# Batch two's v sorted in natural layout and re-tiled through DRAM, with GpSimd holding later loads until x^T is there

## The chip, the cores and the metric

One core of a Trainium2 chip. The metric is the device time of one execution in microseconds (us), as the median of several runs. The kernel before takes 226.36 us (226.34 to 226.47, three runs).

The names in the profiles: PE is TensorE and its matmuls, PEld its weight loads, DVE is VectorE, ACT is ScalarE, POOL is GpSimd, SP is the engine whose queue (the sync queue) issues the other transfers; GpSimd issues the loads. To evict is to copy a matmul's result out of PSUM. A turn, or crossbar transpose, is a DMA that transposes on the way. The granted clock is the share of the full TensorE clock that the trace shows.

## The reference

Block-sorted attention over 4 batches and 8 heads, followed by an FFN with squared ReLU. Cut to what matters:

```python
P = sinkhorn(sort_net)                                  # [B, H, 8, 8], five rounds
k_sorted = einsum('bhij,bhjcd->bhicd', P, k_blocks)     # blocks of 96 tokens, 64 wide
v_sorted = einsum('bhij,bhjcd->bhicd', P, v_blocks)
attn = softmax(q_block @ k_sorted_block.T / 8)          # inside each block of 96
x = (attn @ v_sorted_block)  ->  [3072, 512]            # 4 batches of 768 tokens
out = relu(x @ w_in) ** 2 @ w_out                       # w_in 512x2048, w_out 2048x512
```

## The kernel before

The attention of a batch is interleaved with the FFN of earlier tokens, in an order that a small planner in the program lays out: each piece of work is given engines, an estimated cost and its dependences, and the plan's order becomes the fixed instruction order of each engine. The FFN goes in eight groups of 384 tokens, each of 64 `hp` matmuls (up projection) and 48 `op` matmuls (down projection), or 28 "chunks" of four matmuls. Attention tasks are due at a chunk number.

Batches one and two sort k and v by transposing matmuls and then turn v back with TensorE:

```python
def s_sort(u, t, ...):                 # one tensor of one head pair: 12 matmuls
    nc.tensor.matmul(out=tp[64*h:64*(h+1), a, :], lhsT=src[:, 2*u.hp+h, D*a:D*(a+1)],
                     rhs=w_all[:, H*u.b + 2*u.hp + h, ...])
    ...                                # evict to ksT or vsT (128x768)
def s_vt(u, ...):                      # v alone: 8 transposes, then a copy vs<-vbp
    nc.tensor.transpose(out=vbp[:, n, :], in_=u.vsT[:, ...], identity=ident)
```

Batches three and four sort in natural layout by 32x32 tiles of the array. v then goes to DRAM and back (`v_way`, `vblk`) to get its key blocks; k and q are turned by the DMA crossbar, k from its evicted tile `kn`, q from a copy `qi`:

```python
def s_nat(b, g, t, due):               # one tensor of two head pairs: 16 matmuls
    nc.tensor.matmul(out=p2[slot][32*c:32*(c+1), h, 0:NA*D], lhsT=w_t[r, ...],
                     rhs=src[r, g, NA*D*c:NA*D*(c+1)], tile_position=(r.start, 32*c))
    ...                                # evict to kn (ring of three) or vn; then for v:
    nc.sync.dma_start(out=v_way[b, g]..., in_=vn_r[m]...)
    nc.sync.dma_start(out=vb_r[w]..., in_=v_way[b, g]...)
def s_turn(b, hp):
    nc.sync.dma_start_transpose(out=kx_r[kx]..., in_=kn_r[m]...)
    nc.vector.tensor_copy(out=qi_r[n]..., in_=qkv[b][0][:, 2*hp:2*hp+2, :]...)   # DVE
    nc.sync.dma_start_transpose(out=tiles["qT", b, hp], in_=qi_r[n]...)
```

The inputs of batches three and four are loaded by GpSimd as soon as their buffers (those of two batches before) are free. x^T of batches two to four is made by crossbar too (`xT<-ao`), but for one of batch two's four parts.

The softmax here doesn't subtract the row's maximum and nothing guards it: scores larger than these inputs give would overflow.

## Time and profile before

| | before |
|---|---|
| median of three runs | 226.36 us |
| span of the profiled execution | 224.3 us, granted TensorE clock 1.0 |
| first `hp` matmul starts | 22.3 us |
| last matmul starts | 220.8 us |

### The profile page before, as it was taken

Reading aid. Unit: us, or ns where it says so; the run is one execution under the profiler, and the core shown is the slowest. Engines: PE = TensorE matmul, PEld = TensorE weight load, DVE = VectorE, ACT = ScalarE, POOL = GpSimd, SP = SyncE. Lnnn points to the kernel's source line nnn. Section 1 sums busy time; section 2 is a strip of 40 time slices with the busy share of each in tenths; the row PEclk is TensorE's granted clock in tenths of the full one; section 3 lists DMA queues with packets and bytes.
Section 4 is the critical chain, followed back from the end, with each engine's and each line's share of the span. In section 5 each row is a group of like instructions: output and inputs, shape, how many; then the busy total and the mean of one; then the engine's idle time right before and its main releaser. Section 6 shows DMA issues by size and latency. Waiting matters only on the chain.

```text
span 224.3 us, 5245 instructions
## 1 busy us (share of the span) xinstructions
PE 216.6 (97%) x2130; PEld 122.9 (55%) x2145; DVE 105.7 (47%) x297; ACT 122.1 (54%) x253; POOL 26.4 (12%) x46
## 2 busy tenths in 40 slices
PE   7898999999999999999999999999999999999994
PEld 2476665556665645545665455445665465446553
DVE  6777777317666416640666127523664045005400
ACT  4665776228885328734775248535774177137521
POOL 7962332200004200000000000000000000000000
PEclk9999999999999999999999999999999999999999
DMA  5999999999953996499941320899522410110012
GB/s 66 201 202 208 207 206 205 203 227 245 210 65 27 191 239 145 115 216 201 220 38 35 85 94 0 164 225 254 110 37 43 122 47 1 50 57 37 0 50 94
DMA packets 42744, 28.83 MB, mean 129 GB/s; under 512 B 22752, under 2 KB 38368, under 8 KB 42720
## 3 DMA queue, kind: packets, MB, share of 16 engines
q0 software_dynamic: 13888, 13.63, 37.1%
q1 hardware_dynamic: 28832, 14.86, 29.7%
q8 instruction: 17, 0.28, 0.5%
q14 instruction: 7, 0.06, 0.1%
HBM read 28.89 MB, written 7.91 MB: 164 GB/s over the span
## 4 chain that ended last, share of the span: by engine, by line
PE 92%; DMA 2%; DVE 2%; ACT 1%; issue 1%; ACTq 0%; POOLq 0%
PE hp L810 37%; PE op L838 35%; PE p L550 4%; PE p L731 3%; DMA qb<-in_q_dram 2%; PE p L510 2%; PE qtp L461 2%; PE vbp L598 2%; PE op L872 2%; PE p L350 1%; PE p L632 1%; PE xtp L779 1%; PE tp L510 1%; DVE ao L742 1%; ACT h L818 0%
## 5 line engine op out<-in xcount | busy, mean ns | idle before, releaser
L810 PE MATMUL hp<-xT,w_in_bf 128*128 128x384 bf16 x512 | 91.0, 326 | 0.0
L838 PE MATMUL op<-w_out_bf,h 128*128 128x512 bf16 x353 | 82.6, 379 | 0.8
L818 ACT ACTIVATE h<-hp 128x384 bf16<-128x384 f32 x128 | 62.0, 495 | 23.5 <-PE hp L810 20.0
L821 DVE TENSOR_TENSOR h<-h 128x384 bf16<-128x384 bf16 x128 | 44.5, 355 | 56.3 <-ACT h L818 55.5
L810 PEld LDWEIGHTS <-w_in_bf 128*128 128x128 bf16 x512 | 47.0, 98 | 30.0 <-issue 0.7
L838 PEld LDWEIGHTS <-h 128*128 128x128 bf16 x368 | 34.7, 98 | 39.4 <-issue 0.7
L192 ACT COPY ob<-op 128x512 f32<-128x512 f32 (+1 forms) x25 | 14.2, 569 | 56.0 <-PE op L838 50.6
L742 DVE TENSOR_TENSOR ao<-p,rec 96x512 bf16<-96x512 f32 x32 | 22.0, 687 | 1.4 <-DVE rec L741 0.3
L582 ACT ACTIVATE et<-p 96x384 bf16<-96x384 f32 x48 | 19.4, 491 | 2.4 <-PE p L550 2.4
L741 DVE RECIPROCAL rec<-p 96x8 f32<-96x8 f32 x32 | 6.4, 199 | 13.6 <-PE p L731 13.3
L731 PEld LDWEIGHTS <-et 96*128 96x128 bf16 x256 | 10.6, 97 | 2.9
L261 POOL DMA_DIRECT2D qb<-in_q_dram x8 | 6.0, 754 | 32.5 <-PE qtp L461 24.4
L350 PE MATMUL p<-ones 128*128 128x512 bf16 (+1 forms) x36 | 8.8, 360 | 1.1 <-DVE ones L213 1.1
L194 DVE COPY vs<-vbp 96x512 bf16<-96x512 bf16 (+1 forms) x12 | 6.1, 508 | 7.1 <-PE vbp L598 6.9
L573 ACT ACTIVATE et<-p 96x768 bf16<-96x768 f32 x8 | 6.3, 802 | 2.1 <-PE p L550 2.0
L261 POOL DMA_DIRECT2D kb<-in_k_dram x10 | 6.6, 659 | 6.6 <-DMA w_in_bf<-in_moe_w_in_dram 2.2
L261 POOL DMA_DIRECT2D vb<-in_v_dram x10 | 6.6, 660 | 6.4 <-DMA w_in_bf<-in_moe_w_in_dram 3.6
L192 ACT CAST ksT<-p 128x768 bf16<-128x768 f32 (+1 forms) x7 | 4.6, 662 | 3.3 <-PE p L510 3.3
L550 PEld LDWEIGHTS <-kx 64*128 64x128 bf16 x128 | 4.6, 155 | 2.8 <-issue 2.8
L731 PE MATMUL p<-vs,et 96*128 96x65 bf16 x128 | 6.0, 193 | 0.0
L461 PE MATMUL qtp<-ident,qb 64*64 64x64 bf16 (+1 forms) x144 | 4.7, 204 | 1.3 <-DMA qb<-in_q_dram 1.3
L461 PEld LDWEIGHTS <-qb 64*64 64x64 bf16 (+1 forms) x144 | 3.5, 109 | 4.5 <-DMA qb<-in_q_dram 2.3
(78 smaller groups left out, 129.3 us busy)
## 6 DMA issues: line engine op xcount, KB each, us to landing
out_dram<-ob SPq DMA_DIRECT2D x23, 256.0 KB, 2.8
qb<-in_q_dram POOLq DMA_DIRECT2D x8, 384.0 KB, 15.7
vb<-in_v_dram POOLq DMA_DIRECT2D x6, 384.0 KB, 17.1
kb<-in_k_dram POOLq DMA_DIRECT2D x6, 384.0 KB, 17.1
w_in_bf<-in_moe_w_in_dram POOLq DMA_DIRECT2D x4, 512.0 KB, 12.5
w_out_bf<-in_moe_w_out_dram POOLq DMA_DIRECT2D x4, 512.0 KB, 18.0
v_way<-vn SPq DMA_DIRECT2D x4, 396.0 KB, 4.1
vblk<-v_way SPq DMA_DIRECT2D x4, 396.0 KB, 3.9
```

The lines of the kernel that those rows point to most:

```text
L192: nc.scalar.copy(out=out, in_=in_)
L261: nc.gpsimd.dma_start(out=dst, in_=src)
L350: nc.tensor.matmul(out=out, lhsT=ones, rhs=rhs, start=True, stop=True)
L461: nc.tensor.transpose(out=t["p"][64 * h:64 * (h + 1), a, :], in_=qb[p0:p1, 2 * hp + h, D * a:D * (a + 1)], identity=ident[p0:p1, p0:p1])
L550: nc.tensor.matmul(out=scp[:, h, BLK * n:BLK * (n + 1)], lhsT=(u.ksT[64 * h:64 * (h + 1), hf, BLK * n:BLK * n + 128] if u.b < 2 else kx_r[ ...
L582: nc.scalar.activation(out=et[:, h, 0:HS].rearrange("p (n c a) -> p n c a", c=C0, a=NA), in_=st["p"][0:96, h, 0:HS].rearrange("p (n a c) - ...
L731: nc.tensor.matmul(out=oup[:, h, 66 * n:66 * n + D + 1], lhsT=et_r[u.et[hf]][:, h, BLK * n:BLK * n + 128], rhs=(u.vs[:, NQ * hf + n, h, 0: ...
L742: nc.vector.tensor_tensor(out=u.ao[:, n0:n0 + NQ, :, :].rearrange("p n e d -> p e n d"), in0=ov[:, :, :, 0:D], in1=rec[:, :, :, None].to_b ...
L810: nc.tensor.matmul(out=t["hp", nt][:, 0:HS], lhsT=w_in_bf[:, kc, 128 * nt:128 * (nt + 1)], rhs=xT[:, kc, t0:t0 + HS], start=(kc == 0), sto ...
L818: nc.scalar.activation(out=t["h1", nt], in_=t["hp", nt][:, 0:HS], func=AF.Relu)
L821: nc.vector.tensor_tensor(out=t["h2"][:, nt, :], in0=t["h1", nt], in1=t["h1", nt], op=ALU.mult)
L838: nc.tensor.matmul(out=t["op", mt], lhsT=t["h2"][:, nt, 128 * mt:128 * (mt + 1)], rhs=w_out_bf[:, nt, :], start=(nt == 0), stop=(nt == NT ...
```

## The change

Batch two's v goes the way of batches three and four: natural layout, two tasks of 16 matmuls, DRAM and back. Its loads are reordered for that. GpSimd's order is fixed, and GpSimd reads the last column of x^T of the batch before ahead of the loads of batches three and four, so that no load runs beside the crossbar. The tasks of those batches move 3 and 4 chunks later. The core of the diff (cut: masks, the flat layout of ksT and vsT, the earlier build of w_t, the estimated times of loads and of v's trip):

```diff
-        mybir.EngineType.SP}))
+        mybir.EngineType.SP, mybir.EngineType.Pool}))
...
+    load(1, 2, 0, HP)
     for g in range(4):
         ...                                            # w_out
-    for g in range(2):
-        for t in (2, 1, 0):
-            load(1, t, HP * g, HP)
+    for t, g in ((2, 1), (1, 0), (0, 0), (1, 1), (0, 1)):
+        load(1, t, HP * g, HP)
...
-                u.v_op = s_sort(u, 2, due)
+                if b == 0:
+                    u.v_op = s_sort(u, 2, due)
+            if b == 1 and hp % 2 == 0:
+                todo.append((14 + 2 * hp, len(todo),
+                             lambda due, g=hp // 2: s_nat(1, g, 2, due), b))
...
     def load_late(b):
+        def hold(e):
+            nc.gpsimd.tensor_copy(out=held[0:1, 0:HP - (b == 2), b:b + 1],
+                                  in_=xT[0:1, 0:HP - (b == 2), S * b - 1:S * b])
+        holds[b] = plan.add("POOL", 0.1, hold, [x_done[b - 1, x, 0] for x in range(HP - (b == 2))])
+        landed["last"] = plan.add("DMA", 3.2, lambda e: None, [holds[b]])
...
-    lay_late(2, 2 * n_up)
-    lay_late(3, 4 * n_up)
+    lay_late(2, 2 * n_up + 3)
+    lay_late(3, 4 * n_up + 4)
```

(In the code batches count from 0, so `b == 1` is batch two.)

More of the change, by code (lines that the diff above doesn't have):

```diff
@@ L218 @@
     for n in range(3):
-        for r, name, hs in ((ksT_r, "ksT", 2), (vsT_r, "vsT", 2)):
-            sT = const.tile([128, hs, HS + 32], BF16, name=f"{name}{n}")
-            nc.vector.memset(sT[:, :, HS:HS + 32], 0.0)
+        for r, name in ((ksT_r, "ksT"), (vsT_r, "vsT")):
+            sT = const.tile([128, S + 32], BF16, name=f"{name}{n}")
+            for x in (HS, S):
+                nc.vector.memset(sT[:, x:x + 32], 0.0)
             r.append(sT)
@@ L255 @@
     qkv = {}
+    holds = {}
+    held = const.tile([1, HP, B], BF16)
     landed = {}
@@ L262, in dma @@
         op = plan.add("POOL", 0.75, issue, deps)
-        landed[key] = plan.add("DMA", mb / 0.39, lambda e: None, [op, landed.get("last")])
+        landed[key] = plan.add("DMA", mb / (0.39 if key[0] == 0 else 0.43), lambda e: None, [op, landed.get("last")])
         landed["last"] = landed[key]
@@ L274, in dst_src @@
             alloc_qkv(b)
-            if b > 1 and t:
+            if b > 1 and t or b == 1 and t == 2:
                 return (qkv[b][t].rearrange("p (g h) x -> p g (h x)", h=HP)[:, h0 // HP, :],
@@ L279, in load @@
         dma((b, t, h0, p.start), 1.57 * n / H * (p.stop - p.start) / 128, dst_src,
-            readers[b - 2] + [x_done[b - 1, x, 0] for x in range(HP)] if b > 1 else [])
+            readers[b - 2] + [holds[b]] if b > 1 else [])
     def load_w_in(g):
@@ L292 @@
     mask_t = const.tile([128, 4], BF16)
+    mask_1 = const.tile([128, C0], BF16)
     def make_mask(e):
@@ L300, in make_mask @@
             src, w = dst, w // 2
+        nc.gpsimd.tensor_copy(out=mask_1.rearrange("p (z y) -> p z y", y=4),
+                              in_=mask.rearrange("p (y z) -> p z y", z=4))
     for g in range(HP):
@@ L392, in fn @@
                 out=w_all[:, h0:h0 + n, :, :],
-                in0=mask[:, None, None, :].to_broadcast([128, n, NB, C0]),
+                in0=(mask if h0 < H else mask_1)[:, None, None, :]
+                .to_broadcast([128, n, NB, C0]),
                 in1=s[:, :, h0:h0 + n].rearrange("p i h -> p h i")[:, :, :, None]
@@ L517, in ev @@
         def ev(e):
-            h0 = u.halves[0]
-            copy(e, (u.ksT if t == 1 else u.vsT)[:, h0:h0 + len(u.halves), 0:HS]
-                 .rearrange("p h (x a) -> p h x a", a=NA),
-                 st["p"].rearrange("p a (h x) -> p h x a", x=NQ * C0))
+            dst = u.ksT if t == 1 else u.vsT
+            if u.b == 0:
+                copy(e, dst[:, BLK * u.i0:BLK * (u.i0 + u.ni)]
+                     .rearrange("p (x a) -> p x a", a=NA), st["p"].rearrange("p a x -> p x a"))
+            else:
+                copy(e, dst[:, 0:S].rearrange("p (n a x) -> p n a x", a=NA, x=C0),
+                     st["p"].rearrange("p a (n x) -> p n a x", x=C0))
         h0 = 2 * u.hp
@@ L551, in mm @@
                             out=scp[:, h, BLK * n:BLK * (n + 1)],
-                            lhsT=(u.ksT[64 * h:64 * (h + 1), hf, BLK * n:BLK * n + 128]
+                            lhsT=(u.ksT[64 * h:64 * (h + 1), HS * hf + BLK * n:HS * hf + BLK * n + 128]
                                   if u.b < 2 else
@@ L599, in mm @@
                     out=vbp[:, n, :],
-                    in_=u.vsT[:, i // NQ, BLK * (i % NQ):BLK * (i % NQ) + 128],
+                    in_=u.vsT[:, BLK * i:BLK * i + 128],
                     identity=ident)
@@ L628, in mm @@
                 src = qkv[b][t].rearrange("p (g h) x -> p g (h x)", h=HP)
+                w = w_t[:, HP // 2 * b + g, :, :].rearrange("p c i -> p (c i)")
                 for h in range(2):
@@ L633, in mm @@
                             out=p2[slot][32 * c:32 * (c + 1), h, 0:NA * D],
-                            lhsT=w_t[r, HP // 2 * b + g, :, :].rearrange("p c i -> p (c i)"),
+                            lhsT=w[r, :],
                             rhs=src[r, g, NA * D * c:NA * D * (c + 1)],
@@ L664, in read @@
                 in_=v_way[b, g].rearrange("a (c i) x -> (a c) (i x)", i=NB))
-        wr = plan.add("SP", 0.33, write, evs + [loaded(b)])
-        there = plan.add("WAY", 2.0, lambda e: None, [wr])
+        wr = plan.add("SP", 0.33, write, evs + ([loaded(b)] if b > 1 else []))
+        slow = 6.0 if b == 1 else 2.0
+        there = plan.add("WAY", slow, lambda e: None, [wr])
         rd = plan.add("SP", 0.33, read, [there] + oldw)
-        back = plan.add("WAY", 2.0, lambda e: None, [rd])
+        back = plan.add("WAY", slow, lambda e: None, [rd])
         rvn.use(m, *evs, there)
@@ L674, in loaded @@
     def loaded(b):
-        return [landed[b, t, HP, 0] for t in (0,)][0]
+        return landed[b, 0, HP, 0]
     def s_turn(b, hp):
@@ L716, in s_av @@
         nao, olda = rao.take()
-        if u.b > 1:
+        if u.b > 0:
             w, u.vs_op = v_blk[u.b, u.hp // 2]
@@ L733, in mm @@
                             lhsT=et_r[u.et[hf]][:, h, BLK * n:BLK * n + 128],
-                            rhs=(u.vs[:, NQ * hf + n, h, 0:D + 1] if u.b < 2 else
+                            rhs=(u.vs[:, NQ * hf + n, h, 0:D + 1] if u.b < 1 else
                                  vb_r[w][:, NQ * hf + n, 2 * (u.hp % 2) + h, 0:D + 1]),
@@ L753, in s_av @@
             ret.use(u.et[hf], pe)
-            if u.b < 2:
+            if u.b < 1:
                 rks.use(u.n, pe)
@@ L948, in open_ @@
                 u.k_op = kops[b, hp] = s_sort(u, 1, due)
-                u.v_op = s_sort(u, 2, due)
+                if b == 0:
[3 more added lines that the diff above has]
+                             lambda due, g=hp // 2: s_nat(1, g, 2, due), b))
             for f, s in ((0.0, open_),
                          (0.35, lambda due, box=box: s_sc(box["u"], due)),
-                         (0.5, lambda due, box=box: s_vt(box["u"], due)),
+                         (0.5, lambda due, box=box: b == 0 and s_vt(box["u"], due)),
                          (0.75, lambda due, box=box: s_av(box["u"], due)),
@@ L960, in lay_late @@
         todo.append((c0, len(todo), lambda due: load_late(b), 0))
-        if b == 2:
-            todo.append((c0, len(todo), build_wt, 0))
         for g in range(2):
@@ L985 @@
     lay(0, (1,), 0, n_up)
+    todo.append((8, len(todo), build_wt, 0))
     lay(1, (0, 1), n_up, 2 * n_up)
-    lay_late(2, 2 * n_up)
-    lay_late(3, 4 * n_up)
+    lay_late(2, 2 * n_up + 3)
+    lay_late(3, 4 * n_up + 4)
     for due, _, stage, b in sorted(todo, key=lambda x: x[:2]):
```

## The prediction

> **What bounds the kernel now.** I read the page first: busy shares, the 40 slices, the chain that ended last.
>
> ```profile
> PE 216.6 (97%) x2130; PEld 122.9 (55%) x2145; DVE 105.7 (47%) x297; ACT 122.1 (54%) x253; POOL 26.4 (12%) x46
> ...
> PEclk9999999999999999999999999999999999999999
> DMA  5999999999953996499941320899522410110012
> ```
>
> PE is busy 97% at full clock; no other engine passes 55%. The DMA row is full early, when PE does not wait for it. A busy PE need not be a bound PE, so next came the chain of waits in order of time. These are its pieces for the second and third head pair of the second batch and for the third batch's k and v (columns: start us, length us, what):
>
> ```profile
> 57.00 0.46 PE p L510 x12
> 57.46 0.76 PE hp L810 x4
> 58.22 0.28 PE p L550 x8
> ...
> 58.51 0.35 PE p L550 x8
> 58.86 0.76 PE hp L810 x4
> 59.62 0.45 PE vbp L598 x8
> 60.06 1.30 PE hp L810 x8
> 61.36 0.51 PE p L731 x16
> 61.87 0.65 PE hp L810 x4
> ...
> 88.64 0.31 PE p L632 x16
> 88.95 1.41 PE hp L810 x8
> 90.36 0.31 PE p L632 x16
> ```
>
> From 22 us to 221 us this chain is matmul after matmul (two waits of 0.9 us at the starts of the last two down projections apart), so a microsecond of PE work removed there is a microsecond of span. Four matmuls of the up projection take 0.65 us, or 0.76 us right after a tiled piece: a tiled piece costs its own length plus 0.11 us. The 57.00 piece sorts v of one head pair; 59.62 is the transposes of that v into key blocks; a 0.31 us piece at L632 sorts one tensor of TWO head pairs in natural layout by 32x32 tiles, with no transposes after it. That is how the third and fourth batch already work.
>
> Third, the groups by shape, for the evictions, and the landing times. The q load of the second batch's first half, asked for alone (first line), is issued at 25.2 us and lands after 18.3; the weights w_out (second) land up to 20.5 after their issues from 14.7 to 17.1; the first and the last crossbar transpose alone (third, fourth) take 7.1 and 2.8 us:
>
> ```profile
> L261 POOL DMA_DIRECT2D qb<-in_q_dram x1: 740/740/740, 25.2 to 25.2; - x1
> ...
> DMA to landing us min/median/max: 18.3/18.3/18.3
> ```
>
> ```profile
> L261 POOL DMA_DIRECT2D w_out_bf<-in_moe_w_out_dram x4: 740/746/762, 14.7 to 17.1; - x4
> ...
> DMA to landing us min/median/max: 15.2/18.0/20.5
> ```
>
> ```profile
> L764 SPq DMA_TRANSPOSE xT<-ao x1: 1312/1312/1312, 56.5 to 56.5; - x1
> ...
> DMA to landing us min/median/max: 7.1/7.1/7.1
> ```
>
> ```profile
> L764 SPq DMA_TRANSPOSE xT<-ao x1: 1214/1214/1214, 172.4 to 172.4; - x1
> ...
> DMA to landing us min/median/max: 2.8/2.8/2.8
> ```
>
> Loads and crossbar do slow each other (7.1 against 2.8 us), but no piece of the chain between 22 and 221 us is a DMA.
>
> **What the Trainium skill says.** "TensorEngine Tiling (Array Packing)", section Key Properties: changing the tiling mode drains the array, and tiles work independently. The trace agrees: 0.11 us on the first full matmuls after a tiled piece, and sixteen 384-column matmuls by 32x32 tiles in 0.31 us, where one after the other at 0.65/4 us each they would take 2.6. The same page, section PSUM Bottleneck: tiling speeds the matmul and not the eviction. It agrees: the 128x768 eviction takes 958 ns on DVE and 799 ns on ACT for vn, and 957 and 804 ns for vsT. "DMA: Bandwidth & Descriptors", section Issuing engines are not separate DMA queues: SP's and GpSimd's transfers share the same 16 engines. It agrees, by the 7.1 us transpose beside the loads. The same page, section Two DMAs through the same engine are not ordered: the read of a DRAM scratch must wait for the landing of its write. So the new trip is two full latencies in a row; the group list has 4.1 us for v_way and 3.9 us for vblk.
>
> **The change part by part.**
>
> Removed on PE, second batch, all in the saturated stretch. Sort of v by four head pairs: in the first and fourth pair k and v are one piece (0.67 and 0.80 us for 24 matmuls), so half goes, 0.34 + 0.40. In the second and third v stands alone between up-projection matmuls, 0.46 us plus the 0.11 of the mode change: 2 x 0.57 = 1.14. Transposes of v: pieces of 0.55, 0.45, 0.45 and 0.55 us; where one follows the scores directly its 0.55 holds the mode change that the next matmul will pay instead, so 4 x 0.45 = 1.80. Sum 0.34 + 0.40 + 1.14 + 1.80 = 3.68 us.
>
> Added on PE: two natural-layout sorts, one for two head pairs each, in the first group of the FFN: 2 x (0.31 + 0.11) = 0.84. The fourth such piece of the third batch took 0.53 us, so 1.28 is the upper figure. Net gain 2.4 to 2.8 us.
>
> Moved on PE: the build of w_t (0.16 us at 82.53) comes earlier and costs the same. The tasks of batches three and four come 3 and 4 FFN chunks later; their number stays.
>
> DVE and ACT lose four evictions of v by head pair against four of vn at the same price, and four copies vs<-vbp of 687 ns. Neither engine is on the path: nothing on the span. Six more memsets at the start: DVE starts them every 0.03 to 0.09 us and has 0.53 us of idle before its first reduction, so about 0.36 us is hidden. The extra mask copy on GpSimd is about 0.2 us (its sibling fold took 213 ns) between loads whose queue is behind anyway (issue to landing 7 us): hidden.
>
> Loads: v's first half of batch two goes ahead of w_out. A 384 KB load takes about 2 us in the stream (landings of that stretch are 1.9 us apart), so w_out's last quarter lands at 37.6 + 2 = 39.6 us. It is first needed in the fourth group of four down matmuls, at 41.3 before, 41.7 with the new piece: hidden. The second half of v lands near 41.6. The first half of q lands at 25.2 + 18.3 = 43.4 before, so 45.4 after, plus what the new scratch transfers take of the engines: three of 396 KB at some 1.5 us (an estimate, 3.9 us issue to landing less the 2 us that a lone store needs) makes 49 to 50. It is needed at 49.4 + 0.84 = 50.3: barely hidden. Sorted v itself is written near 37 us and back by 49 even at 6 us a way; its first use is at 54: hidden.
>
> Hold: batch three's loads, before at 35 to 63 us, start after the third transpose, about 72 us, and at 2.3 us each (the burst at 70.6 us before) are in by 89; its first sort is at 88.6 and needs only the first two, in by about 80. Batch four's start after about 127.5; its first k and v land near 133 and 135, its first sort comes at 137.4: hidden with 4 us. The hold makes the transposes of batch two about 4 us faster, off the path: worth nothing in time.
>
> End of batch four: its last attention matmul ended at 170.86, the transpose landed at 172.4 + 2.8 = 175.2, and the up projection that reads it began at 179.49, ten chunks later. Four chunks later leaves 6 x 0.865 = 5.2 us for a way of 4.4: hidden with 0.8.
>
> Sum: 226.36 - 2.6 = 223.8 us.
>
> **The rivals.**
>
> (1) q or k of batch two becomes the wait at about 50 us, since the scratch transfers, v and the stores meet there. For: the DMA row is full, and the margin is 0 to 1 us. Against: batch three's loads leave this stretch, though they stand behind in the queue. It would cost 0.5 to 1.5 us: 224.5 to 225.3.
>
> (2) The hold puts late loads onto the path: batch four's k or v lands after its place in PE's order, and PE, which works in order, stands. For: some 60 us of slack before shrinks to 4. Against: the loads have the DMA engines nearly alone there (share 0.21 from 121 to 137 us before). It would cost 1 to 3 us: 225 to 227.
>
> (3) Batch four's last transpose, given only 5.2 us, arrives late behind a store on the sync queue: plus 0.3 to 1, so 224.1 to 224.8.
>
> (4) PE time removed is given back as idle, because scores, exponentials and the next matmul now have less between them (the transposes used to fill that 0.45 us). For: four exponentials of 491 ns stand behind each pair's scores. Against: the FFN's matmuls fill whatever is free. At most 4 x 0.45: 225.6.
>
> (5) Quicker transposes let PE run ahead, below 222. Nothing in the chain waits for them; I give this little.
>
> **Range and chances.** The sum is 223.6 to 224.0; the rivals, each at one in eight to one in four, pull up. I say 223.8, with 222.9 to 225.3 eight times in ten. 2% would be 4.5 us, beyond the whole 3.7 us that is removed: faster by over 2% 0.03; slower by over 2% needs two of the rivals at their worst: 0.02; within 2% 0.95.
>
> **What would show it right or wrong.** Right: no vsT or vbp piece in the chain between 50 and 78 us; two more L632-type pieces of 0.31 us before 45 us; PE busy down by about 2.6 us with its idle unchanged; four fewer vs copies of 96x1024; batch two's transposes near 3 us. Wrong: a piece of the chain that is a DMA or a wait near 38 to 50 us (rival 1), near 136 to 146 (rival 2) or before the seventh up projection (rival 3), or L632 pieces well over 0.5 us; above all, a chain whose first 22 us have changed, where I predict nothing.

## More of the kernel before

The prediction shows the busy shares and the chain. What I use beside it is the table of stretches. This is its answer for the kernel before, cut where the first, second, third, fifth and seventh FFN group start: stretch; its length; then busy time and number of instructions of PE, PEld, DVE, ACT and POOL; granted clock; DMA share; GB/s.

```profile
22.27:50.52 28.25, 28.09 (x321) 16.18 (x317) 15.32 (x41) 14.51 (x29) 7.32 (x11) 1.00 1.27 210
50.52:82.61 32.09, 31.89 (x393) 19.23 (x392) 18.22 (x41) 19.60 (x42) 3.62 (x6) 1.00 0.88 159
82.61:130.98 48.37, 48.16 (x417) 26.20 (x417) 22.51 (x57) 27.25 (x58) 0.00 (x0) 1.00 0.66 135
130.98:179.33 48.35, 48.14 (x413) 26.18 (x416) 22.08 (x56) 27.30 (x58) 0.00 (x0) 1.00 0.53 116
```

The reader is to see lengths and not busy times: each stretch holds the same FFN work in both kernels (one group in the first two, two groups in the others), so a difference in length between two kernels is attention work or waiting. The first stretch has the rest of batch one, the second batch two, the third and fourth batches three and four.

## The result, and the profile after

The changed kernel takes 226.05 us (225.63 to 226.26, four runs) beside 226.41 (226.34 to 226.47) for the kernel before. The ratio is 0.9982, with a 95% interval of 0.9965 to 0.9999. A ratio here is the mean time of one kernel's runs over that of the other's of the same rounds, so not quite the ratio of the medians quoted. Executions over 1.5% slower than the fastest of the same kernel are left out of the means. I had predicted 223.8, in 222.9 to 225.3. The gain is 0.4 us where 2.6 was expected, and the interval only just excludes no gain at all.

The same table of stretches, of the changed kernel, cut at the same FFN groups:

```profile
22.13:51.73 29.60, 29.49 (x346) 16.25 (x341) 16.67 (x43) 16.02 (x31) 3.50 (x5) 1.00 1.22 218
51.73:80.13 28.40, 28.40 (x324) 16.43 (x321) 14.41 (x37) 17.58 (x38) 3.82 (x7) 1.00 0.51 107
80.13:129.25 49.12, 48.64 (x417) 26.21 (x416) 21.59 (x56) 26.79 (x58) 1.04 (x3) 1.00 0.79 149
129.25:178.56 49.31, 48.78 (x417) 26.23 (x416) 22.50 (x57) 26.69 (x57) 2.76 (x5) 1.00 0.85 162
```

Against before: +1.35 where the two new sorts are, -3.69 in batch two, then +0.75 and +0.96 in batches three and four. At the start of the third group the changed kernel is 2.48 us ahead (80.13 against 82.61). The expected gain was there, and was given back later.

The chain of waits of the changed kernel says in whose hands it was lost. First the second head pair of batch two, to answer the pieces shown of before; then what surrounds the two later stretches' losses:

```profile
57.42 0.46 PE p L518 x12
57.88 1.41 PE hp L823 x8
59.28 0.45 PE p L561 x16
59.73 1.41 PE hp L823 x8
61.13 0.65 PE p L744 x16
...
73.45 9.67 DMA qb<-in_q_dram
83.14 0.63 DVE qi L708 x2
83.77 0.28 DVE h L834
84.13 0.50 ACT h L831
84.67 4.06 PE hp L823 x24
...
139.31 0.88 DVE kn L194
140.23 0.35 PE p L644 x8
...
142.14 4.97 DMA kx<-kn
147.23 0.97 DVE kn L194
148.25 0.35 PE p L644 x8
```

No v sort (the 57.00 piece before) and no transposes stand between the up projections any more; the L518 piece here is k's sort. But from 67 us on the chain is no longer PE's: it goes through the last crossbar transpose of batch two, for which the hold waits, and from 73 us through a DMA. The load of q, issued after the hold, lands at 83.1 us. DVE has two copies of q (`qi`) next in its order and stands there; behind them stand the squares of the FFN; behind those ACT's ReLU, whose buffers are not freed; behind those PE. The view of waits puts numbers to it (engine and line, releaser: us in all, times, longest):

```profile
DVE qi L708 <- DMA qb<-in_q_dram: 7.9, 2, 6.6
DVE kn L194 <- DMA kx<-kn: 5.0, 1, 5.0
```

DVE stood 6.6 us in one piece, and PE stood idle for 0.48 us of it. PE was in a down projection until 80.1 us, and then six outputs of the up projection (24 matmuls) still found room in three buffers for ReLU and three in PSUM. The same happened in batch four: q landed at 138.1 us, the eviction of k came late, and PE's sorts were torn apart by waits at 139.5 and 147.7 us. The second of these has one more link, the `kx<-kn` piece: v's store, ahead in the sync queue, waited for v's late eviction, so the turn of k went out at 142.1 us, and the fourth eviction of k needs the buffer that this turn gives back. In start-to-start time, the v sorts of that batch went from 0.85 to 1.81 us, which is all of the +0.96.

So theory A: the hold makes q late, and q's copies, at a fixed place in DVE's order, carry that to PE. Rivals: PE waits for late k and v directly (B), or the tasks moved later are what costs (C).

### The profile page after: what moved, and what is told of

Read it like the earlier page. It is cut to its first block, busy times and chain, and to the rows that moved or that the text cites. A ratio compares the mean times of both kernels' runs of the same rounds, so it can differ in the third digit from the quotient of the medians.

```text
span 224.2 us, 5181 instructions
## 1 busy us (share of the span) xinstructions
PE 216.7 (97%) x2097; PEld 120.5 (54%) x2097; DVE 102.6 (46%) x300; ACT 120.4 (54%) x252; POOL 26.6 (12%) x49
## 4 chain that ended last, share of the span: by engine, by line
PE 64%; DMA 13%; DVE 9%; issue 5%; ACT 4%; POOL 2%; POOLq 0%; SPq 0%; ACTq 0%; DVEq 0%
PE hp L823 27%; PE op L851 24%; DMA qb<-in_q_dram 8%; DVE ao L755 3%; PE p L561 3%; DMA xT<-ao 3%; PE p L744 2%; DMA kx<-kn 2%; ACT h L831 2%; PE op L885 2%; PE p L644 1%; PE p L518 1%; ACT et L593 1%; PE vbp L609 1%; PE tp L518 1%
## 5 line engine op out<-in xcount | busy, mean ns | idle before, releaser
L851 PE MATMUL op<-w_out_bf,h 128*128 128x512 bf16 x368 | 83.6, 379 | 0.0
L831 ACT ACTIVATE h<-hp 128x384 bf16<-128x384 f32 x128 | 60.6, 497 | 22.1 <-PE hp L823 15.2
L834 DVE TENSOR_TENSOR h<-h 128x384 bf16<-128x384 bf16 x128 | 43.7, 354 | 54.9 <-ACT h L831 54.0
L192 ACT COPY ob<-op 128x512 f32<-128x512 f32 (+1 forms) x23 | 13.0, 567 | 58.3 <-PE op L851 52.8
L357 PE MATMUL p<-ones 128*128 128x512 bf16 (+1 forms) x36 | 9.8, 395 | 1.1 <-DVE ones L213 1.1
L744 PE MATMUL p<-vblk,et 96*128 96x65 bf16 x192 | 8.3, 193 | 0.0
L194 DVE CAST kn<-p 128x768 bf16<-128x768 f32 x4 | 3.8, 957 | 8.8 <-DMA kx<-kn 5.0
L708 DVE COPY qi<-qb 128x768 bf16<-128x768 bf16 x8 | 2.7, 355 | 11.0 <-DMA qb<-in_q_dram 7.9
L194 DVE CAST vn<-p 128x768 bf16<-128x768 f32 x6 | 5.7, 957 | 3.3 <-PE p L644 3.3
## 6 DMA issues: line engine op xcount, KB each, us to landing
vb<-in_v_dram POOLq DMA_DIRECT2D x6, 384.0 KB, 12.5
```

Source lines behind the costliest of these rows:

```text
L192: nc.scalar.copy(out=out, in_=in_)
L194: nc.vector.tensor_copy(out=out, in_=in_)
L357: nc.tensor.matmul(out=out, lhsT=ones, rhs=rhs, start=True, stop=True)
L744: nc.tensor.matmul(out=oup[:, h, 66 * n:66 * n + D + 1], lhsT=et_r[u.et[hf]][:, h, BLK * n:BLK * n + 128], rhs=(u.vs[:, NQ * hf + n, h, 0: ...
L831: nc.scalar.activation(out=t["h1", nt], in_=t["hp", nt][:, 0:HS], func=AF.Relu)
L834: nc.vector.tensor_tensor(out=t["h2"][:, nt, :], in0=t["h1", nt], in1=t["h1", nt], op=ALU.mult)
```

## The experiments

### Without the hold

```diff
         def hold(e):
-            nc.gpsimd.tensor_copy(out=held[...], in_=xT[...])
+            pass
```

> The changed kernel, with GpSimd's two reads of x^T taken out and nothing else; PE, DVE, ACT and SP keep the very same order of instructions, so only the time at which the loads of batches three and four start is altered. Theory A (the hold makes the q loads land after DVE has come to the copies of q, the squares of the FFN stand behind those copies, and PE stands behind the squares): the waits near 84, 139.5 and 147.7 us go, 226.05 becomes 224.8 (224.4 to 225.1). Rival B (PE waits for the late k and v loads themselves): the same here. Rival C (the tasks moved 3 and 4 chunks later cost the time, not the hold): stays at 226.0. Transposes of batch two slow down to 6 to 7 us beside loads in all theories.

Measured: 229.10 us (227.49 to 230.22), ratio 1.0106 (1.0085 to 1.0128). A miss in the total, and both halves of it are of use. The third and fourth stretch became 48.47 and 48.37 us, so the losses there are gone, as A and B had said and C had not: the hold causes them, not the moved tasks. But batch two's stretch took 34.42 us in place of 28.40. The chain there, and the stretches around the wait:

```profile
46.90 12.06 DMA vblk<-v_way
...
59.09 1.04 PE p L744 x16
60.13 0.78 PE qtp L469 x12
```

```profile
51.72:59.40 7.68, 4.28 (x47) 2.49 (x44) 1.41 (x4) 4.44 (x10) 0.00 (x0) 0.90 1.14 251
59.40:67.00 7.60, 7.60 (x75) 4.38 (x73) 3.30 (x9) 4.26 (x9) 0.00 (x0) 0.65 1.14 246
```

With batch three's loads in the DMA queues from 39.8 us on, the return of v from DRAM takes 12.1 us against 6.8 in the changed kernel. In this profiled execution, the slowest of the six, PE stands 3.4 us, and then its granted clock falls to 0.65 over the 7.6 us window, so that it loses another 2.6 us without any wait. I had put the hold's worth at nothing; to v's new way it is worth 6.0 us here. (The mean clock of 0.985 in this execution is that fall; the other runs, 0.991 to 0.998, have no trace.)

### The copies of q on GpSimd

```diff
-            nc.vector.tensor_copy(out=qi_r[n]..., in_=qkv[b][0]...)
+            nc.gpsimd.tensor_copy(out=qi_r[n]..., in_=qkv[b][0]...)
...
-        qp = plan.add("DVE", 0.5, q_pair, ...)
+        qp = plan.add("POOL", 1.2, q_pair, ...)
```

> The changed kernel with the hold, but the eight copies of q into head pairs run on GpSimd instead of DVE; PE, ACT and SP keep the same order. Theory A: DVE no longer stands before the squares, the PE wait at 84 us goes and most of those at 139.5 and 147.7; 226.05 becomes 224.9 (224.6 to 225.3). Rival B (k and v themselves late): no gain, 226.0. Rival C: 226.0.

Measured: 224.38 us (224.22 to 224.51), ratio 0.9911 (0.9898 to 0.9923). The loads land when they did (q at 83.4 us; GpSimd now stands 7.3 us for it), PE's order is the same, and the chain has:

```profile
80.45 7.80 PE hp L823 x48
```

where the changed kernel had 24 matmuls, a wait, and 24. The third stretch is 48.47 us, the fourth 48.50: 0.65 and 0.81 us back. This decides for A and against B, in the changed kernel. Of the 1.71 us lost there, 0.25 stay: 0.10 in the third stretch, which the run without any hold has too (48.47), so it goes with the moved tasks, and 0.15 in the fourth, nearly all of it in the v sorts (0.98 us for 0.85), where DVE still stands 4.7 us for the buffer of k. Of the 1.7 us gained, 1.3 are earlier matmuls; the rest is in the closing part, told below.

### An honest load rate in the planner

```diff
-landed[key] = plan.add("DMA", mb / (0.39 if key[0] == 0 else 0.43), ...)
+landed[key] = plan.add("DMA", mb / (0.39 if key[0] == 0 else 0.31 if key[0] in (2, 3) else 0.43), ...)
```

> The changed kernel with the hold, but the planner that lays out the engines' orders is told the load rate that the trace shows for batches three and four (0.31 MB a us in place of 0.43), so it puts the copies of q three to four squares later in DVE's order. Theory A: part of the loss comes back, 225.3 (224.9 to 225.7). Rival B: 226.0. Rival C: 226.0.

Measured: 227.04 us (226.48 to 228.59), ratio 1.0039 (1.0015 to 1.0063). A miss: slower than the change. The losses that A speaks of did go (third stretch 48.47; v sorts of batch four 0.85 us). But the planner now also puts batch four's turns later in the sync queue: in the profiled execution, the fastest of the six, a turn of q issued at 153.2 us lands 5.5 us later, and PE's scores wait for it, idle for 1.6 us from 157.3. One wait was exchanged for another, now for a turn of q: the third stretch agrees with A, the total decides nothing, and the slower executions have no trace.

### The hold alone

The kernel before, with GpSimd's order fixed, the hold, its estimated rates and the 3 and 4 chunks; v as before.

```diff
+            nc.gpsimd.tensor_copy(out=held[...], in_=xT[...])     # ahead of batch three's and four's loads
-    lay_late(2, 2 * n_up)
-    lay_late(3, 4 * n_up)
+    lay_late(2, 2 * n_up + 3)
+    lay_late(3, 4 * n_up + 4)
```

> The kernel before with the hold, the later tasks and the fixed GpSimd order alone; v of batch two as before by the transposed sort. Theory A: no PE work is saved and the waits of the changed kernel come in, 226.4 becomes 227.5 (227.0 to 228.0). If the loss in the changed kernel came from v's new way through DRAM instead, this stays at 226.4.

Measured: 230.22 us (229.94 to 230.66), ratio 1.0171 (1.0158 to 1.0184). The direction is right and the size is not: 3.8 us lost, not 1.1. Third stretch 49.73 us, fourth 51.19. PE stands idle for 1.5 us and 0.9 us, until 144.1 and 152.9, in the same places as in the changed kernel. Here the hold lets go later (132.1 us against 128 for batch four), since batch two's PE work is longer. I took the excess for the same mechanism; two runs below show that this was not the whole of it.

### Only the first hold; a hold on v's way; and both with q's copies on GpSimd

If the hold's worth is v's way, it should be enough to hold batch three's loads until v is back, near 57 us. Four kernels were run together; the fourth was a control on the kernel before.

```diff
 # only the first hold
+            if b == 3:
+                return
             nc.gpsimd.tensor_copy(out=held[...], in_=xT[...])
```

> The changed kernel with GpSimd's first read of x^T (ahead of batch three's loads) kept and the second (ahead of batch four's) taken out; the order on PE, DVE, ACT and SP stays the same. Theory A: the 3.70 us that the second batch's stretch won stay won, the 0.5 us wait near 84 us stays, the waits near 139.5 and 147.7 us go: 226.05 becomes 225.1 (224.8 to 225.4). If instead batch four's loads do harm beside batch three's crossbar transposes and its v trip at 83 to 111 us, a new wait comes there and it is 226 or more.

```diff
 # batch three's loads wait for v's return; batch four's for nothing (w, back and the planned gap are cut)
-            nc.gpsimd.tensor_copy(out=held[...], in_=xT[...])
-        holds[b] = plan.add("POOL", 0.1, hold, [x_done...])
+            nc.gpsimd.tensor_copy(out=held[0:1, 0, 0:1], in_=vb_r[w][0:1, 0, 0, 0:1])
+        holds[b] = None
+        if b == 2:
+            holds[b] = plan.add("POOL", 0.1, hold, [back])
```

> The changed kernel with GpSimd reading, ahead of batch three's loads, the first element of v's key blocks of batch two as they come back from DRAM (near 57 us) instead of x^T, and no hold ahead of batch four's. If what the hold protects is v's trip through DRAM (theory D, from the run without any hold, where PE waited 3.7 us for that trip and its granted clock then fell), all waits go: loads from 57 us are in by 73, so 224.1 (223.8 to 224.5). If it is the crossbar that has to be kept free of loads (what the change says it is for), transposes of batch two at 58, 63 and 69 us slow to 7 us and PE waits for them: 226 or more.

The control, the kernel before with q's copies on GpSimd:

> A control: the kernel before, with the copies of q on GpSimd instead of DVE. There those copies wait for no load when DVE comes to them. Theory A: nothing is won, 226.4 (226.2 to 226.8). If DVE's load itself were the cost, it would gain as much as in the changed kernel, some 1.5 us: 224.9.

And v's way as the hold, with q's copies on GpSimd:

> The hold on v's way back, and the copies of q on GpSimd, both. Theory A with D: with the loads early, no copy of q waits, so the second change adds nothing: the same as the hold on v's way alone, 224.1 (223.8 to 224.5). If it is faster than that by over 0.3 us, some wait on DVE was left.

(The 3.7 us in the text of the hold on v's way runs from the start of the matmul before; PE's idle time was 3.4.)

Measured, in this order: 237.88 us (237.13 to 240.08), ratio 1.0522; 243.46 over all six runs, the three fast 238.39, 241.16 and 241.34, ratio 1.0614; 226.15 (226.12 to 226.25), ratio 0.9990; 236.56 over all, three fast runs of 232.58 to 235.58, ratio 1.0317. Three misses, by loads beside turns each time. The chain of the kernel with only the first hold:

```profile
85.20 19.05 DMA qT<-qi
...
104.34 0.36 DVE qi L708
...
104.75 0.37 DVE h L834
...
105.17 3.17 PE op L851 x7
```

One crossbar turn of q takes 19 us. Batch four's loads were issued from 76.2 us and landed until 106.6, so they ran beside batch three's turns (the first three took 13.6, 19.1 and 16.6 us; 2.6 to 4.4 in batch four, with no load about). With the hold on v's way alone, batch four's loads are in the queues from 69.6 us, and the turns of q, which the planner has now put at 73.7 and 77.9 us, take 21.5 and 18.9. In both kernels the copies of q on DVE wait for the turn to give back one of two buffers, the squares wait behind them, PE stands idle (3.2 and 6.7 us in the first, 12.5 us in the second), and its clock falls to half.

With the copies on GpSimd the squares go on, but the turns of k stand behind those of q in the sync queue, the first until 103.8 us, and PE stands 6.1 us for a `kn` buffer; this kernel is some 7 us faster than the one without that move, so DVE's order was part of the loss and not all of it. With v's way as the hold, in both kernels, PE also stood idle at 80.6 us, for 1.2 and 2.2 us, until the last crossbar transpose of batch two landed, which took 12.9 and 13.9 us beside the loads of both batches. The third stretch of the three is 11.6 to 16.9 us longer than the 48.47 without waits.

So the hold's stated aim, to keep loads from the crossbar, is a real one. My reading after the first run, that it only protects v's way, was wrong; that run had escaped by luck of order, its turns of q at 87 us taking 7 to 8 us beside the last of the loads. The kernel before escaped because all its loads had landed by 88 us and its turns began at 92. The control did what A said: no wait for q in the kernel before, and no gain in PE's time.

### v's way for batch three, x^T for batch four

```diff
         def hold(e):                                       # (the dependences are cut)
+            if b == 2:
+                nc.gpsimd.tensor_copy(out=held[0:1, 0, 0:1], in_=vb_r[w][0:1, 0, 0, 0:1])
+                return
             nc.gpsimd.tensor_copy(out=held[...], in_=xT[...])
```

> The changed kernel, where GpSimd waits ahead of batch three's loads for v's return from DRAM (near 57 us) and ahead of batch four's, as in the change, for x^T. Against the run with the hold on v's way alone it differs in batch four's hold only. If that run lost its time to batch four's loads beside batch three's crossbar turns (21 us for one turn), and batch three's loads beside batch two's three transposes do no harm, the wait near 84 us goes and those near 139.5 and 147.7 stay: 226.05 becomes 225.3 (224.9 to 225.7). If loads beside batch two's transposes are what costs, 228 or more.

> The same, with the copies of q on GpSimd. Theory A: the last waits go as well; no better than the change with those copies on GpSimd and its own holds (224.38), since that one had no wait left: 224.4 (224.1 to 224.7).

Measured: 225.21 us (225.10 to 225.71), ratio 0.9950 (0.9937 to 0.9963); with q's copies on GpSimd 224.52 (224.09 to 225.26), ratio 0.9918 (0.9905 to 0.9931). Both as expected. Batch three's loads beside batch two's x^T transposes cost nothing here: the transposes took 7.3 to 12.4 us, but the last landed at 76.3 us, and their first reader, batch two's FFN, starts at 80.2. The third stretch is 48.47 us in both; the fourth is 49.53, and 48.51 with the copies moved. So the hold for batch three may let go 15 us earlier than the change has it; the hold for batch four may not be dropped.

### Why the hold alone costs more

> The kernel before with the hold alone (230.22), and the copies of q on GpSimd. Theory A: nearly all of the 3.8 us that the hold cost there passes through those copies on DVE, so 226.7 (226.3 to 227.3). If the hold costs by the lateness of k and v, or by later turns, it stays above 229.

The edit is that of the copies of q, on the kernel with the hold alone. Measured: 230.34 us (228.59 to 231.51), ratio 1.0170. A miss: A alone does not explain that kernel. The third stretch came back to 48.72 us, but the fourth went to 52.24. The chain shows what stood in for q:

```profile
148.92 0.34 PE p L634 x8
149.26 1.04 issue
150.30 0.97 DVE kn L194
151.31 0.35 PE p L634 x8
```

The fourth eviction of sorted k needs one of the three `kn` buffers, and the first of them is given back when its crossbar turn lands: issued at 143.7 us beside the last of the held loads, landed at 150.2. PE stands idle for 2.1 us (2.4 from the start of one half of the v sort to that of the other), and seven of its down matmuls after that start 427 ns apart in place of 216. So I gave the ring a fourth buffer:

```diff
-    kn_r = [const.tile([128, NA, 2, D], BF16, name=f"kn{n}") for n in range(3)]
+    kn_r = [const.tile([128, NA, 2, D], BF16, name=f"kn{n}") for n in range(4)]
...
-    rkx, rkn, rqi = Ring(3), Ring(3), Ring(2)
+    rkx, rkn, rqi = Ring(3), Ring(4), Ring(2)
```

> The kernel before with the hold alone and the copies of q on GpSimd (230.34), with four buffers for sorted k instead of three; all engines keep their order. If the 2.4 us wait at 148.9 us and the lower granted clock after it come from the fourth eviction of k, which waits until the crossbar turn of the first, slowed by the late loads, gives its buffer back, they go: 226.8 (226.4 to 227.4). If the turn is awaited elsewhere too, it stays above 228.5.

Measured: 226.24 us (226.12 to 226.30), ratio 0.9992 (0.9978 to 1.0005); the fourth stretch is 48.38 us. With the two in-order hand-overs taken away, the copies of q and the ring of k, the hold costs nothing that can be measured. The late loads of k and v themselves (B) were not what PE waited for.

### The closing part

In the changed kernel the span ends 4.19 us after the start of the last matmul, in the kernel before 3.55. In its closing barrier GpSimd's record has a gap of 0.4 us before its 69th traced instruction; so have the three other programs with 69 or 70 of them. Eight one-element copies on GpSimd, after its last load, move that place into idle time:

```diff
+    def pad(e):
+        for n in range(8):
+            nc.gpsimd.tensor_copy(out=held[0:1, n % HP, n // HP:n // HP + 1], in_=mask_t[0:1, 0:1])
+    plan.add("POOL", 0.8, pad, [landed["last"]])
```

> The changed kernel with eight one-element copies on GpSimd after its last load, in time that it has free; all other engines keep their order. If the gap of 0.4 us in the closing barrier belongs to GpSimd's 69th instruction wherever that falls, it moves into idle time: last matmul to end 3.8 us instead of 4.2, and 226.05 becomes 225.65 (225.4 to 225.9). If it belongs to the barrier, 226.05 stays.

Measured: 225.61 us (225.49 to 226.03), ratio 0.9969 (0.9957 to 0.9982), last matmul to end 3.79 us. The intervals of the two ratios overlap, so the trace decides: the gap is gone from the closing barrier, and from the last matmul to the end of the execution it is 5.59 us and not 5.95. The gap belongs to the place in GpSimd's program. The kernel before has 66 such instructions and meets it too, it seems, after the span's end: its profiled execution took 226.45 us for a span of 224.33, 2.12 more, where all the programs with 78 or more have 1.76 to 1.85 more. So this 0.4 us is no loss of the change, only one that shows in its span. From the start of the last matmul to the end of the execution it is 5.67 us before and 5.95 after; these 0.28 us are a loss. What the gap is, no run shows.

## Why the prediction was wrong, point by point

- **v's sort and transposes, 3.68 us.** Right: in start-to-start time of the matmuls, over the whole kernel, they are 3.84 us less.
- **The new sorts, 0.84 to 1.28.** Right: 0.91 us. The first piece took 0.59 and not 0.31 us. Of the rest of the first stretch's +1.35, 0.16 us is the build of w_t, which moved there from the second, and some 0.3 is spread over small terms. The two stretches gain 2.34 us, for 2.4 to 2.8 predicted: a little short.
- **v's trip hidden, back by 49 us.** Right in the result, wrong in its size: 6 us a way was assumed and 9.5 and 6.8 measured, so it was back at 53.7 us, 1.8 before its reader, and not at 49. The run without the hold shows that this slack is the hold's doing.
- **"The hold ... worth nothing in time", and late loads "hidden with 4 us".** This is the step that failed. I asked only when k and v would be needed, and k and v did come in time. I left out the q copies, which stand in DVE's order ahead of the FFN's squares. q landed at 83.1 and 138.1 us, DVE stood 6.6 and 1.3 us for it, and the two stretches lost 1.71 us. Moving the copies to GpSimd gave back 1.46 us of PE time (0.65 and 0.81). And the hold is worth something: 6.0 us to v's trip, and 11.6 us and more to the turns that come after, when loads run beside them.
- **Rival 2** named the hold and 225 to 227 us, and the outcome lies in it; but it named k and v, and the runs show q on DVE instead, and behind it the ring of k.
- **Rivals 1, 3, 4 and 5** did not happen. Batch two's first q landed at 46.5 us and not at 49 to 50, 4.5 before its reader. The last x^T transpose landed at 178.0 us, 0.6 before its reader.
- **The signs.** The missing pieces of v, the two new sorts, the missing copies and the transposes near 3 us (2.8 to 3.2) all came. PE's busy time did not fall by 2.6 us: 216.6 us before, 216.7 after. The stretches show the gain and the loss; this sum does not.
- **The first 22 us** did not change: -0.14 us, where the first `hp` matmul of kernels that start as the changed one does comes between 22.12 and 22.30 us. **The end** did, by the 0.28 us above.

The terms for the pair of profiled executions: -0.14 - 2.34 + 0.75 + 0.96 = -0.77 us at the last matmul, plus 0.28 at the end, makes -0.49 (226.45 to 225.96). Over all runs it is -0.4.

The best version that was run is the change with the copies of q on GpSimd: 224.38 us, ratio 0.9911; with v's way as batch three's hold as well it is the same within the noise (0.9918).

## What to carry to other kernels

When a transfer is put off, look for every instruction that waits for it on any in-order engine, and ask what stands behind that instruction; a cheap copy on an engine at 46% held up the one at 97%. A hold that looks idle may be what keeps a DRAM trip or a crossbar turn short, so take it away in a run before calling it worthless. And read the lengths of stretches with equal work, not busy shares: here the shares were the same before and after, while 2.3 us were won and 1.7 lost.

## What the Trainium skill lacked or had wrong

- "DMA: Bandwidth & Descriptors", section Rules for kernel authors, says that a transpose next to ordinary DMAs needs nothing. For the result, which that row is about, it held in all runs here. For the time it is not so: an x^T transpose took 2.8 us alone and 7.1 beside loads, and a turn of q 18.9 to 21.5 us beside a full queue of loads. The page has no such figure.
- Not a lack, but the fact that I missed: "TensorE: Matmul & The Clock Gate" says in the table at its head that ScalarE, VectorE and GpSimdE take instructions in strict order, and that TensorE may pull weight loads ahead. The run with the copies moved agrees: the same loads at the same time, and 1.46 us of PE time less.
- The same page, section Why this matters for your kernels, warns of gaps of over some 3 us between matmuls. After a wait of 3.4 us the granted clock was 0.65 over 7.6 us, which agrees. But after waits of 2.1 us (the hold alone with the copies moved) and 2.2 us (v's way as the hold, with the copies moved) the clock was 0.5 for 3.4 us, so here a shorter gap was enough; after waits of 1.5 and 1.6 us in two other kernels it stayed at 1.0.
- No page has the gap of 0.4 us before GpSimd's 69th instruction, which cost the changed kernel 0.36 us between last matmul and end (5.95 to 5.59 with eight more instructions before it).
